# A fused attention and two-layer MoE kernel on Trainium2: other transfers for the token units, and half of MoE 2's weight preparation moved into its first pass

## The chip, the cores and the metric

The kernel runs on one core of a Trainium2 chip. The metric is the device time of one execution in microseconds (us) on that core; lower is better. Engines are named as in the profile: PE (TensorE), DVE (VectorE), ACT (ScalarE), POOL (GpSimd), SP (SyncE, which here issues DMA transfers; POOL issues some as well).

## The reference

Batch 4, 8 heads, 576 tokens, head dimension 64. Cut to what is computed:

```python
# attention: softmax over tokens pooled by 4 and repeated, plus a local softmax with |i - j| < 4
attn = np.repeat(sm_attn(q_d, k_d, v_d), 4, axis=2) + local_attn(q, k, v)
x = attn.transpose(0, 2, 1, 3).reshape(2304, 512)
# MoE 1: w_gate and w_val are 512 x 1536, w_out 1536 x 512
x = (1 / (1 + np.exp(-(x @ w_gate))) * (x @ w_val)) @ w_out
# MoE 2: w_in is 512 x 2048, w_out 2048 x 512
h = x @ w_in
g = h * np.tanh(np.log1p(np.exp(np.minimum(h, 20.0))))   # log1p(..) is h above 20
out = g @ w_out
```

## The kernel before, in words

**Numbers.** Weights are read as 64-bit numbers and narrowed to fp32 on the chip: a raw tile is loaded (`load64`), POOL or ACT makes `rebias` (L181, L179), DVE narrows in three steps (L189, L192, L196). An fp32 operand is split into `hi`, a rounded part (ACT copy, L219), and `lo`, the rest (a subtraction, L222); a product of two split operands is three matmuls.

**Blocks.** MoE 1 is done in four blocks, one per batch. Block b runs the gate and value products of batch b (`m1`, L1008 to 1010, result in `sg`, L1014) and its output products (`m1out`), and weaves in the attention of batch b + 1 (tokens come in as `tok` and `vw`) and steps of weight preparation. A planner (`weave`) sets that order, with costs, dependencies and due times: in blocks 1 and 2 a job for MoE 2's output weights (`o2`) falls due every 9500 ns, each narrowing 128 x 512 numbers, splitting them and storing both parts to `wd2` (`park_o2`); in block 3 a job for MoE 2's input weights (`i2`) every 4500 ns, 16 in all. An `i2` job also makes three sums of its quarters on POOL (L1233) and is split as 128 x 896; the jobs of the first four quads (u < `NQ`) stay in the tile `wi`, the others go to `wi2d` in device memory.

**Token units.** From four quarters of MoE 1's output, `m1out` makes seven units by additions and subtractions, for two halves `c2` of the features. `unit_out` copies a unit to `hi`, subtracts it in place to `lo`, and stores each to device memory: 256 columns to `x2d`, all batches side by side in one tensor, and, for six of the seven units, 32 rest columns to `x2r`. That is 28 + 24 stores a block. The units of `c2` = 0 lie in `stage` and a `sg` tile (`sx`), those of `c2` = 1 have their `hi` in `G`. The tiles of MoE 2 (`xu3`, `xu4`, `wo`, `g2`, `r`, `hs`, `v`) lie where `R`, `stage` and `G` were.

**MoE 2.** With seven units on each side, the product with `w_in` takes seven products instead of eight (`product`, L1332 to 1334, in the order 1, 5, 6, 2, 7, 3, 4 into `h`). MoE 2 makes two passes over halves of its hidden features: `order` is batches 0 to 3 and then the rest columns of all batches (REST, four products), and in the second pass REST first and the batches back to 0. A phase (L1395) does the products of one batch for two quads, with `mish` (L1352 to 1358) and `put_g`; between them it puts, as `units`, the output matmuls `m2out` (`po`, L1345 to 1347) of the batch before. `finish` (L1381 to 1391) stores the partial result to `pd` in the first pass; in the second it loads that into one of two `r` tiles, adds and stores the output. `follow` (L1464) loads a unit `xu` of the next batch right after its last use. `load_x2` (L1263), `load_o2` (L1253) and `load_wi` (L1256) issue on POOL's queue. `units2` (L1284) releases the pool of the weight jobs and loads the first five units of batch 0, after the last `i2` job; `xu3` and `xu4` and the `wo` tiles are loaded after block 3.

**Order.** On each engine instructions run in the order in which they stand; a scheduler lays that order out from the program's order and dependencies.

## Time and profile before

| what | us |
|---|---|
| three runs, median (lowest to highest) | 1065.14 (1056.53 to 1067.11) |
| the profiled execution | 1063.76 |
| its span, first to last instruction | 1062.0 |

The mean granted clock of PE in the profiled execution was 0.976 of full speed. Times in the rows are counted from the span's start. Blocks 0 to 3 run from about 110, 235, 380 and 525 us, MoE 2 from 652, its second pass from about 871. The time between two instructions of an engine is named idle and carries, in brackets, what released it.

### The profile page before, as it was taken

Reading aid. Unit: us, or ns where it says so; the run is one execution under the profiler, and the core shown is the slowest. Engines: PE = TensorE matmul, PEld = TensorE weight load, DVE = VectorE, ACT = ScalarE, POOL = GpSimd, SP = SyncE. Lnnn points to the kernel's source line nnn. Section 1 sums busy time; section 2 is a strip of 40 time slices with the busy share of each in tenths; the row PEclk is TensorE's granted clock in tenths of the full one; section 3 lists DMA queues with packets and bytes.
Section 4 is the critical chain, followed back from the end, with each engine's and each line's share of the span. In section 5 each row is a group of like instructions: output and inputs, shape, how many; then the busy total and the mean of one; then the engine's idle time right before and its main releaser. Section 6 shows DMA issues by size and latency. Waiting matters only on the chain.

```text
span 1062.0 us, 20544 instructions
## 1 busy us (share of the span) xinstructions
PE 988.1 (93%) x7914; PEld 920.6 (87%) x7914; DVE 694.8 (65%) x1050; ACT 578.6 (54%) x1307; POOL 340.0 (32%) x380
## 2 busy tenths in 40 slices
...
GB/s 201 178 126 221 216 193 197 180 230 237 190 214 165 164 174 169 195 172 92 146 226 159 218 270 259 293 92 172 80 99 99 139 352 151 112 217 68 152 40 100
DMA packets 165794, 184.85 MB, mean 174 GB/s; under 512 B 71104, under 2 KB 131264, under 8 KB 165184
## 3 DMA queue, kind: packets, MB, share of 16 engines
...
## 4 chain that ended last, share of the span: by engine, by line
PE 62%; DMA 15%; DVE 8%; ACT 5%; POOL 4%; issue 3%; SPq 3%; ACTq 0%; DVEq 0%; POOLq 0%
PE po L1345 6%; PE po L1347 6%; PE po L1346 6%; PE ps_m L1008 6%; PE h L1332 5%; PE h L1334 5%; PE h L1333 5%; PE ps_m L1009 5%; PE ps_m L1010 5%; PE ps_o L1052 2%; PE ps_o L1054 2%; PE ps_o L1056 2%; DMA d<-wd 2%; DMA x2d<-stage 2%; DVE R L222 2%
## 5 line engine op out<-in xcount | busy, mean ns | idle before, releaser
L1008 PE MATMUL ps_m<-R 128*128 128x288 f32 (+2 forms) x768 | 235.2, 308 | 5.7 <-DVE sg L1014 4.1
L1009 PE MATMUL ps_m<-R 128*128 128x288 f32 (+2 forms) x768 | 232.1, 302 | 2.3 <-POOL R L222 2.3
L1010 PE MATMUL ps_m<-R 128*128 128x288 f32 (+2 forms) x768 | 231.1, 301 | 0.0
L1332 PE MATMUL h<-xu,R 128*128 128x256 f32 x512 | 146.8, 287 | 13.2 <-DMA xu<-x2d 11.0
L1008 PEld LDWEIGHTS ps_m<-R 128*128 128x128 f32 x768 | 147.1, 192 | 11.2 <-DVE sg L1014 5.7
L1009 PEld LDWEIGHTS ps_m<-R 128*128 128x128 f32 x768 | 147.6, 192 | 4.0 <-POOL R L222 2.5
L1010 PEld LDWEIGHTS ps_m<-R 128*128 128x128 f32 x768 | 147.5, 192 | 1.4 <-issue 1.1
L1333 PE MATMUL h<-xu,R 128*128 128x256 f32 x512 | 146.4, 286 | 0.0
L1334 PE MATMUL h<-xu,R 128*128 128x256 f32 x512 | 146.1, 286 | 0.0
L219 ACT CAST R<-d 128x512 fp32r<-128x512 f32 (+1 forms) x152 | 95.5, 634 | 62.6 <-DVE d L214 15.9
L1052 PE MATMUL ps_o<-G,R 128*128 128x288 f32 x384 | 116.0, 302 | 0.3 <-ACT R L219 0.2
L1332 PEld LDWEIGHTS h<-xu,R 128*128 128x128 f32 x512 | 99.4, 194 | 18.4 <-DMA xu<-x2d 6.1
L1054 PE MATMUL ps_o<-G,R 128*128 128x288 f32 x384 | 114.2, 298 | 0.0
L1056 PE MATMUL ps_o<-G,R 128*128 128x288 f32 x384 | 113.5, 298 | 0.0
L1345 PE MATMUL po<-wo,g 128*128 128x512 f32 x288 | 113.2, 394 | 0.0
L1346 PE MATMUL po<-wo,g 128*128 128x512 f32 x288 | 112.7, 391 | 0.0
L1347 PE MATMUL po<-wo,g 128*128 128x512 f32 x288 | 111.0, 394 | 0.0
L222 DVE TENSOR_TENSOR R<-d,R 128x512 fp32r<-128x512 f32 (+1 forms) x118 | 90.2, 769 | 28.0 <-ACT R L219 27.2
L1333 PEld LDWEIGHTS h<-xu,R 128*128 128x128 f32 x512 | 99.5, 194 | 4.4
L1334 PEld LDWEIGHTS h<-xu,R 128*128 128x128 f32 x512 | 99.2, 194 | 0.1
L1265 POOL DMA_DIRECT2D xu<-x2d x52 | 38.9, 749 | 184.2 <-PE h L1334 177.3
L181 POOL TENSOR_SCALAR rebias<-raw 128x512 f32<-128x512 f32 x32 | 58.3, 1822 | 103.5 <-DVE d L196 80.2
...
## 6 DMA issues: line engine op xcount, KB each, us to landing
d<-wd SPq DMA_DIRECT2D x54, 512.0 KB
xu<-x2d POOLq DMA_DIRECT2D x52, 512.0 KB, 4.5
raw<-in_moe_w_out_dram SPq DMA_DIRECT2D x28, 512.0 KB
wd<-d SPq DMA_DIRECT2D x18, 512.0 KB
raw<-in_moe_w_in_dram SPq DMA_DIRECT2D x16, 512.0 KB
wo<-wd POOLq DMA_DIRECT2D x16, 512.0 KB, 6.7
...
```

The costliest lines, as they stand in the source:

```text
L1008: PE.matmul(p[:, 0:n], lhsT=wh, rhs=xh[:, c, ts], start=(c == 0), stop=False)
L1009: PE.matmul(p[:, 0:n], lhsT=wh, rhs=xl[:, c, ts], start=False, stop=False)
L1010: PE.matmul(p[:, 0:n], lhsT=wl, rhs=xh[:, c, ts], start=False, stop=(c == KD - 1))
L1052: PE.matmul(p[:, 0:SUB], lhsT=hi[:, o:o + 128], rhs=gt[:, f, 0, ts], start=(f == 0), stop=False)
L1054: PE.matmul(p[:, 0:SUB], lhsT=hi[:, o:o + 128], rhs=gt[:, f, 1, ts], start=False, stop=False)
L1056: PE.matmul(p[:, 0:SUB], lhsT=lo[:, o:o + 128], rhs=gt[:, f, 0, ts], start=False, stop=(f == KF1 - 1))
L1332: PE.matmul(o, lhsT=wh, rhs=x[:, c, 0, :], start=(start and k == 0 and c == 0), stop=False, skip_group_check=True)
L1333: PE.matmul(o, lhsT=wh, rhs=x[:, c, 1, :], start=False, stop=False, skip_group_check=True)
L1334: PE.matmul(o, lhsT=wl, rhs=x[:, c, 0, :], start=False, stop=(c == 1), skip_group_check=True)
L1345: PE.matmul(p, lhsT=gh, rhs=w[:, 0, :], start=(f == 0), stop=False)
L1346: PE.matmul(p, lhsT=gh, rhs=w[:, 1, :], start=False, stop=False)
L1347: PE.matmul(p, lhsT=gl, rhs=w[:, 0, :], start=False, stop=(f == 2 * NQ - 1))
```

## The change

The tensor `x2d` becomes one tensor per batch with 288 columns a unit, and `x2r` goes. For `c2` = 0, `hi` and `lo` of a unit are stored in one transfer each (14); for `c2` = 1 both are written side by side into `G` and stored in one (7). In blocks 1 and 2 the planner gets four `o2` jobs instead of eight, with a gap of 19000, in block 3 eight `i2` jobs instead of 16, with a gap of 8000. The other eight of each become `jobs`, done in turn by `tick`, which every product of the first pass calls: a raw tile is loaded at the fourth tick, and from the ninth on each tick does one step (rebias; narrow and next load; sums; park). They work in a new pool `sp`. The loads of `wo`, `wi` and `xu` are issued by SP; only the first seven `xu` loads of batch 0 stay on POOL. A unit of rest columns is loaded by eight transfers of 128 x 4 x 32 from the batches' tensors. The last output loop runs `a` outside `f`, with a `finish` after each `a`.

```diff
-    x2d = dram.tile([7, 128, 2, 2, B * T2], F32, name="x2d")
-    x2r = dram.tile([3, 128, 2, 2, 2, B * REM], F32, name="x2r")
+    x2d = [dram.tile([7, 128, 2, 2, SUB], F32, name="x2d%d" % b) for b in range(B)]
...
-    def unit_out(b, c2, i, d, hi):
+    def unit_out(b, c2, i, d, hi, lo):
         ACT.copy(out=hi, in_=d)
-        lo = d.bitcast(F32R)
         DVE.tensor_tensor(out=lo, in0=d, in1=hi.bitcast(F32), op=ALU.subtract)
-        for z, t in enumerate((hi, lo)):
-            t = t.bitcast(F32)
-            SP.dma_start(out=x2d[i - 1][:, c2, z, b * T2:(b + 1) * T2], in_=t[:, 0:T2])
-            if i in KIND:
-                kd, T = KIND[i]
-                SP.dma_start(out=x2r[kd][:, c2, z, T, b * REM:(b + 1) * REM], in_=t[:, T2:SUB])
...
                 h = fpool.tile([128, SUBM], F32R, tag="sg", name="sx")[:, 0:SUB]
-            else:
-                a = g6 + dd[0] * SUB
-                h = G[0][:, a:a + SUB]
-                dd[0] += 1
-            unit_out(b, c2, i, d, h)
+                unit_out(b, c2, i, d, h, d.bitcast(F32R))
+                for z, t in enumerate((h.bitcast(F32), d)):
+                    SP.dma_start(out=x2d[b][i - 1][:, c2, z, :], in_=t)
+                return
+            a = g6 + dd[0] * 2 * SUB
+            dd[0] += 1
+            h = G[0][:, a:a + 2 * SUB]
+            unit_out(b, c2, i, d, h[:, 0:SUB], h[:, SUB:2 * SUB])
+            SP.dma_start(
+                out=x2d[b][i - 1][:, c2, :, :], in_=h.bitcast(F32).rearrange("p (z t) -> p z t", z=2)
+            )
...
-    def park_o2(j, d):
-
-        hi = fpool.tile([128, 512], F32R, tag="rebias", name="hi")
-        split(d, hi, d.bitcast(F32R), DVE, late=True)
-        SP.dma_start(out=wd2[j, :, 0, :], in_=hi.bitcast(F32))
+    def src_o2(j):
+        return w2_out[j * 128:(j + 1) * 128, :].rearrange("(j p) f -> p j f", p=128), 1
+
+    def src_i2(i):
+        u, x = divmod(i, 2)
+        w = w2_in[x * 256:(x + 1) * 256, u * 256:(u + 1) * 256]
+        return w.rearrange("(j p) f -> p j f", p=128), 2
+
+    def park_o2(j, d, hi=None):
+
+        if hi is None:
+            hi = fpool.tile([128, 512], F32, tag="rebias", name="hi")
+        split(d, hi.bitcast(F32R), d.bitcast(F32R), DVE, late=True)
+        SP.dma_start(out=wd2[j, :, 0, :], in_=hi)
         SP.dma_start(out=wd2[j, :, 1, :], in_=d)
...
         done_at[0, "free"] = done_at["start"] = 0.0
-        per = KF2 // 2
+        per = KF2 // 4
         for b in range(B - 1):
...
             if b:
-                srcs = [
-                    (w2_out[j * 128:(j + 1) * 128, :].rearrange("(j p) f -> p j f", p=128), 1)
-                    for j in range((b - 1) * per, b * per)
-                ]
+                srcs = [src_o2(j) for j in range((b - 1) * per, b * per)]
                 extra += narrow_steps(
                     ("o2", b), srcs, clock[0] + 1000.0,
-                    lambda i, d, b=b: park_o2((b - 1) * per + i, d), 9500.0,
+                    lambda i, d, b=b: park_o2((b - 1) * per + i, d), 19000.0,
                 )
...
         def split_i2(i):
-            d = d7s.pop(i)
             u, x = divmod(i, 2)
-            if u < NQ:
-                split(d, wi[:, u, x, 0, :], wi[:, u, x, 1, :], DVE, late=True)
-                return
-            hi = a3.tile([128, UW], F32, tag="hi7", bufs=2, name="hi7")
+            split(d7s.pop(i), wi[:, u, x, 0, :], wi[:, u, x, 1, :], DVE, late=True)
+
+        def park_i2(i, d, hi):
+            u, x = divmod(i, 2)
             split(d, hi.bitcast(F32R), d.bitcast(F32R), DVE, late=True)
...
         def load_o2(h, j):
-            POOL.dma_start(out=wo_at[j], in_=wd2[h * 8 + j].rearrange("p z f -> p (z f)"))
+            SP.dma_start(out=wo_at[j].bitcast(F32), in_=wd2[h * 8 + j].rearrange("p z f -> p (z f)"))
         def load_wi(q):
-            POOL.dma_start(
-                out=wi[:, q].rearrange("p c z f -> p (c z f)"), in_=wi2d[q]
+            SP.dma_start(
+                out=wi[:, q].bitcast(F32).rearrange("p c z f -> p (c z f)"), in_=wi2d[q]
             )
...
-        def load_x2(t, i):
+        def load_x2(t, i, queue=SP):
             if t < B:
-                POOL.dma_start(
-                    out=xu[i - 1].rearrange("p (y t) -> p y t", y=4),
-                    in_=x2d[i - 1].rearrange("p c z t -> p (c z) t")[:, :, t * T2:(t + 1) * T2],
+                dst = xu[i - 1] if queue is POOL else xu[i - 1].bitcast(F32)
+                queue.dma_start(
+                    out=dst.rearrange("p (y t) -> p y t", y=4),
+                    in_=x2d[t][i - 1].rearrange("p c z t -> p (c z) t")[:, :, 0:T2],
                 )
             elif i <= 3:
-                POOL.dma_start(out=xu[i - 1], in_=x2r[i - 1].rearrange("p c z s t -> p (c z s t)"))
-
-        srcs = [
-            (w2_in[x * 256:(x + 1) * 256, u * 256:(u + 1) * 256].rearrange("(j p) f -> p j f", p=128), 2)
-            for u in range(FF2 // 256) for x in range(2)
-        ]
+                dst = xu[i - 1].bitcast(F32).rearrange("p (y s b t) -> p y s b t", y=4, s=2, b=B)
+                for u, (kd, T) in KIND.items():
+                    if kd == i - 1:
+                        for b in range(B):
+                            queue.dma_start(
+                                out=dst[:, :, T, b, :],
+                                in_=x2d[b][u - 1].rearrange("p c z t -> p (c z) t")[:, :, T2:SUB],
+                            )
+
         extra = weights(B - 1)
+        srcs = [src_i2(i) for i in range(2 * NQ)]
         ns = len(srcs)
-        extra += narrow_steps(("i2",), srcs, clock[0], sums_i2, 4500.0, to_i2, ahead=2)
+        extra += narrow_steps(("i2",), srcs, clock[0] + 2000.0, sums_i2, 8000.0, to_i2, ahead=2)
         for i in range(ns):
...
                 xu[i - 1] = a4[0].tile([128, XU], F32R, name="xu%d" % i)
-                load_x2(0, i)
+                load_x2(0, i, POOL)
...
         g2 = m2.tile([128, NQ * 4 * 2 * T2], F32R, name="g2")
+        sp = tc.alloc_tile_pool(name="sp", bufs=1, side="left", reuse_waits="tile")
         g2 = g2.rearrange("p (q s z t) -> p q s z t", q=NQ, s=4, z=2)
...
         for i in (3, 4):
-            load_x2(0, i)
+            load_x2(0, i, POOL)
         for j in range(2):
...
+        jobs = [z for i in range(2 * NQ) for z in ((park_i2, src_i2, 2 * NQ + i), (park_o2, src_o2, 2 * NQ + i))]
+        side, ticks = [], [0]
+        held = {}
+
+        def side_load(k):
+            held["raw"] = load64(*jobs[k][1](jobs[k][2]), sp)
+
+        def side_rebias(k):
+            held["g"] = rebias(held["raw"], POOL, sp)
+
+        def side_narrow(k):
+            held["d", k] = sp.tile([128, UW], F32, tag="d7", bufs=2, name="d7")
+            narrow(held["raw"], held["d", k][:, 0:512], held["g"])
+            if k + 1 < len(jobs):
+                side_load(k + 1)
+
+        def side_sums(k):
+            if jobs[k][0] is park_i2:
+                sums_i2(None, held["d", k])
+
+        def side_park(k):
+            hi = sp.tile([128, UW], F32, tag="hi7", name="hi7")
+            fn, _, i = jobs[k]
+            n = UW if fn is park_i2 else 512
+            fn(i, held.pop(("d", k))[:, 0:n], hi[:, 0:n])
+
+        for k in range(len(jobs)):
+            if k:
+                side.append([lambda k=k: side_park(k - 1), lambda k=k: side_rebias(k)])
+            else:
+                side.append([lambda: side_rebias(0)])
+            side.append([lambda k=k: side_narrow(k)])
+            side.append([lambda k=k: side_sums(k)])
+        side.append([lambda: side_park(len(jobs) - 1)])
+
+        def tick():
+            ticks[0] += 1
+            if ticks[0] == 4:
+                side_load(0)
+            if ticks[0] > 8 and side:
+                for fn in side.pop(0):
+                    fn()
+
         n_y = [0]
...
                     follow(k)
+                    tick()
                     if k > 1:
...
                 follow(i)
+                tick()
...
             prev = (h, t)
-        for f in range(2 * NQ):
-            for a in range(4):
+        for a in range(4):
+            for f in range(2 * NQ):
                 m2out(prev[1], f, a)
-        for a in range(4):
             finish(prev[0], prev[1], a)
```

How instructions stand now. On SP in block 1, the place where batch 2's `tok` tiles are loaded while the last units of batch 1 are stored; before, the end of it:

```order
L358 DMA tok<-in_k_dram 128x8x64
L1035 DMA x2d<-G 128x256
L1038 DMA x2r<-G 128x32
L1035 DMA x2d<-G 128x256
L1035 DMA x2d<-stage 128x256
L1038 DMA x2r<-stage 128x32
L1035 DMA x2d<-stage 128x256
L1038 DMA x2r<-stage 128x32
L1038 DMA x2r<-G 128x32
L1035 DMA x2d<-stage 128x256
L1038 DMA x2r<-stage 128x32
L1035 DMA x2d<-G 128x256
```

and with the change (`x2d_85` is batch 1's tensor):

```order
L1080 DMA x2d_85<-G 128x576 x2
L357 DMA tok<-in_k_dram 128x8x64
L1080 DMA x2d_85<-G 128x576
L249 DMA d<-wd 128x1024
L1080 DMA x2d_85<-G 128x576 x2
L357 DMA tok<-in_q_dram 128x8x64
L1080 DMA x2d_85<-G 128x576 x2
L357 DMA tok<-in_k_dram 128x8x64
L357 DMA tok<-in_q_dram 128x8x64
```

Before, 18 stores stand between a `k` and the next `q` load (the piece shows the first 11); now three.

On POOL at the start of MoE 2, before: the `xu` loads of batch 0 (units 1, 5, 6, 2, 7, then 3 and 4), the last subtractions of the units (`stage`), and `wo`:

```order
L1265 DMA xu_8327<-x2d 128x4x256
L1265 DMA xu_8329<-x2d 128x4x256
L1265 DMA xu_8331<-x2d 128x4x256
L1265 DMA xu_8333<-x2d 128x4x256
L1265 DMA xu_8335<-x2d 128x4x256
L1075 TENSOR_TENSOR stage<-stage 128x256
L1075 TENSOR_TENSOR stage<-stage 128x32
L1075 TENSOR_TENSOR stage<-stage 128x256 x2
L1265 DMA xu_8409<-x2d 128x4x256
L1265 DMA xu_8410<-x2d 128x4x256
L1253 DMA wo_8416<-wd_83 128x1024
L1253 DMA wo_8417<-wd_83 128x1024
```

With the change:

```order
L1269 DMA xu_7673<-x2d_84 128x4x256
L1269 DMA xu_7675<-x2d_84 128x4x256
L1269 DMA xu_7677<-x2d_84 128x4x256
L1269 DMA xu_7679<-x2d_84 128x4x256
L1269 DMA xu_7681<-x2d_84 128x4x256
L1067 TENSOR_TENSOR stage<-stage 128x256 x2
L1067 TENSOR_TENSOR stage<-stage 128x32
L1067 TENSOR_TENSOR stage<-stage 128x256 x4
L1067 TENSOR_TENSOR stage<-stage 128x32
L1067 TENSOR_TENSOR stage<-stage 128x256 x2
L1269 DMA xu_8047<-x2d_84 128x4x256
L1269 DMA xu_8048<-x2d_84 128x4x256
```

The five loads now stand ahead of all subtractions of block 3, where before they stood ahead of the last four.

On SP the same place with the change; the last stores of block 3 (`x2d_87`), the `wo` loads (they read `wd2`, printed as `wd_83`), the first raw tile of the side jobs and batch 1's `xu` loads:

```order
L1080 DMA x2d_87<-G 128x576 x7
L1256 DMA wo_8054<-wd_83 128x1024
L1256 DMA wo_8055<-wd_83 128x1024
L168 DMA raw<-in_moe_w_in_dram 128x2x512
L1256 DMA wo_8056<-wd_83 128x1024
L1256 DMA wo_8057<-wd_83 128x1024
L1256 DMA wo_8058<-wd_83 128x1024
L1256 DMA wo_8059<-wd_83 128x1024
L1256 DMA wo_8060<-wd_83 128x1024
L1256 DMA wo_8061<-wd_83 128x1024
L1269 DMA xu_7673<-x2d_85 128x4x256
L1269 DMA xu_7677<-x2d_85 128x4x256
```

None of these stood on SP before; the `wo` and `xu` loads come from POOL's queue, the raw tile from block 3's jobs.

On PE the last twelve matmuls, before (`po_8435` to `po_8438` are the four outputs):

```order
L1345 MATMUL po_8435<-wo7_8423,g2_8424 128x512
L1346 MATMUL po_8435<-wo7_8423,g2_8424 128x512
L1347 MATMUL po_8435<-wo7_8423,g2_8424 128x512
L1345 MATMUL po_8436<-wo7_8423,g2_8424 128x512
L1346 MATMUL po_8436<-wo7_8423,g2_8424 128x512
L1347 MATMUL po_8436<-wo7_8423,g2_8424 128x512
L1345 MATMUL po_8437<-wo7_8423,g2_8424 128x512
L1346 MATMUL po_8437<-wo7_8423,g2_8424 128x512
L1347 MATMUL po_8437<-wo7_8423,g2_8424 128x512
L1345 MATMUL po_8438<-wo7_8423,g2_8424 128x512
L1346 MATMUL po_8438<-wo7_8423,g2_8424 128x512
L1347 MATMUL po_8438<-wo7_8423,g2_8424 128x512
```

and with the change:

```order
L1355 MATMUL po_8078<-wo7_8061,g2_8062 128x512
L1356 MATMUL po_8078<-wo7_8061,g2_8062 128x512
L1356 MATMUL po_8079<-wo4_8058,g2_8062 128x512
L1354 MATMUL po_8079<-wo5_8059,g2_8062 128x512
L1355 MATMUL po_8079<-wo5_8059,g2_8062 128x512
L1356 MATMUL po_8079<-wo5_8059,g2_8062 128x512
L1354 MATMUL po_8079<-wo6_8060,g2_8062 128x512
L1355 MATMUL po_8079<-wo6_8060,g2_8062 128x512
L1356 MATMUL po_8079<-wo6_8060,g2_8062 128x512
L1354 MATMUL po_8079<-wo7_8061,g2_8062 128x512
L1355 MATMUL po_8079<-wo7_8061,g2_8062 128x512
L1356 MATMUL po_8079<-wo7_8061,g2_8062 128x512
```

Before, the four outputs end three matmuls apart; now the third ends ten before the fourth.

## Rows read from the trace of the kernel before

**Rows 1.** Busy time, share and instructions of each engine, from the page.

```profile
PE 988.1 (93%) x7914; PEld 920.6 (87%) x7914; DVE 694.8 (65%) x1050; ACT 578.6 (54%) x1307; POOL 340.0 (32%) x380
```

**Rows 2.** Waits of PE: line, tile, releaser: us in total, times, longest.

```profile
PE h L1332 <- DMA xu<-x2d: 11.0, 2, 5.7
...
PE ps_t L449 <- DMA tok<-in_q_dram: 6.6, 2, 3.7
...
PE ps_m L1008 <- DVE sg L1014: 4.1, 6, 1.3
```

**Rows 3.** Stretches: PE, PEld, DVE, ACT, POOL busy (instructions), PE clock, DMA share, GB/s.

```profile
400.00:405.00 5.00, 5.00 (x29) 4.80 (x29) 1.19 (x3) 2.40 (x5) 0.00 (x0) 0.66 1.12 279
540.00:595.00 55.00, 50.39 (x364) 48.30 (x363) 50.22 (x82) 28.58 (x59) 39.59 (x41) 1.00 0.50 163
...
652.00:660.00 8.00, 2.64 (x12) 2.26 (x11) 0.95 (x2) 0.82 (x2) 5.75 (x8) 0.81 1.07 264
...
689.00:695.00 6.00, 5.95 (x30) 5.96 (x31) 1.23 (x1) 1.96 (x3) 0.17 (x1) 0.55 1.80 346
...
700.00:871.00 171.00, 171.00 (x1053) 153.18 (x1052) 94.45 (x90) 91.86 (x113) 18.74 (x29) 1.00 0.45 137
```

**Rows 4.** SP's DMA issues from 380 to 396: start, us, line, transfer.

```profile
380.39 0.55 SPq L1035 DMA_DIRECT2D x2d<-stage  x1
...
395.38 0.41 SPq L358 DMA_DIRECT2D tok<-in_q_dram  x1
```

**Rows 5.** Groups by line and shape: busy, mean ns, idle before and releasers.

```profile
L181 POOL TENSOR_SCALAR rebias<-raw 128x512 f32<-128x512 f32 x32 | 58.3, 1822 | 103.5 <-DVE d L196 80.2 <-DVE sum L495 10.8 <-DMA raw<-in_moe_w_in_dram 6.7
...
L1233 POOL TENSOR_TENSOR d<-d 128x128 f32<-128x128 f32 x64 | 45.0, 724 | 21.0 <-DVE d L196 16.4 <-PE ps_m L1010 2.7 <-ACT R L219 1.1
...
L189 DVE TENSOR_SCALAR d<-rebias 128x512 int32<-128x512 int32 x38 | 22.4, 590 | 16.7 <-DMA wd<-d 11.0 <-POOL R L222 2.7 <-ACT rebias L179 1.4
...
L192 DVE SCALAR_TENSOR_TENSOR d<-raw,d 128x512 int32<-128x512 int32 x38 | 30.7, 808 | 0.3
...
L222 DVE TENSOR_TENSOR d<-d,hi 128x896 fp32r<-128x896 f32 x8 | 8.9, 1118 | 3.4 <-ACT hi L219 3.2
...
L222 DVE TENSOR_TENSOR d<-d,hi 128x512 fp32r<-128x512 f32 x16 | 11.1, 691 | 12.5 <-ACT hi L219 12.5
```

**Rows 6.** PE's timeline at MoE 2's first product and at batch 1's first.

```profile
657.77 0.55 PE L1332 MATMUL h<-xu,R 128*128 128x256 f32 x1 [5.36 <-DMA xu<-x2d]
...
689.05 0.58 PE L1332 MATMUL h<-xu,R 128*128 128x256 f32 x1 [5.68 <-DMA xu<-x2d]
```

**Rows 7.** POOL's timeline around the start of MoE 2.

```profile
652.57 3.91 POOL L1265 DMA_DIRECT2D xu<-x2d  x5 [2.11 <-DMA wi2d<-d]
...
680.10 1.65 POOL L1253 DMA_DIRECT2D wo<-wd  x3 [12.03 <-DVE e L1354]
```

**Rows 8.** The chain that ended last, 668 to 698: start, us, what.

```profile
668.63 10.84 DMA x2d<-stage
...
695.03 0.12 PE h L1333
...
697.54 0.23 PE po L1346
```

**Rows 9.** Timeline of the end: PE's last matmul and DVE's last add.

```profile
1054.06 0.39 PE L1347 MATMUL po<-wo,g 128*128 128x512 f32 x1
...
1057.96 0.69 DVE L1389 TENSOR_TENSOR o<-po,r 128x512 f32<-128x512 f32 x1 [0.60 <-DMA r<-pd]
```

**Rows 10.** DVE's split into G, 530 to 610, then 380 to 525: min/median/max ns.

```profile
L222 DVE TENSOR_TENSOR G<-sg,G x21: 439/704/891, 541.2 to 609.8; 128x288 fp32r<-128x288 f32 x21
...
L222 DVE TENSOR_TENSOR G<-sg,G x24: 405/450/1469, 387.8 to 491.5; 128x288 fp32r<-128x288 f32 x24
```

**Rows 11.** Issues of `vw` on SP (ns), and loads of the rest columns (us to landing).

```profile
L378 SPq DMA_DIRECT2D vw<-in_v_dram x80: 595/608/2015, 5.3 to 471.4; - x80
...
xu<-x2r POOLq DMA_DIRECT2D x3, 512.0 KB, 3.6
```

10 lines of the change are left out of this document (6 added, 4 removed).

## Prediction

> **What bounds the kernel now.** I read the page's busy times first, then the waits of PE, then the stretches, and last the timelines of the places where PE stood. PE is busy 988.1 us of a span of 1062.0 [rows 1], so the change can win only the other 74 us, plus what PE runs at the lower of its two clock levels. The waits of PE name three places that this change touches [rows 2]: token loads of attention (6.6 us in two waits), the first MoE's matmuls behind DVE's `sg` (4.1 us in six), and MoE 2's first products behind `xu` loads (11.0 us in two). The stretches [rows 3] show the rest. From 540 to 595 DVE is busy 50.2 of 55 us and PE only 50.4. Around the start of MoE 2 PE does 2.64 us of work in 8 (652 to 660), and from 689 to 695 it is fully busy at a granted clock of 0.55, near 1.2 GHz instead of 2.4. In MoE 2's first pass (700 to 871) PE never stops, with DVE busy 94.45 of 171, 55%: there nothing can be won and something can be lost.
>
> **The change part by part.** The sum is made against the profiled execution, 1063.8 us (span 1062.0); the median of the three runs is 1065.1, the lowest 1056.5.
>
> *Fewer, longer unit stores.* A block issued 28 + 24 stores and now issues 21; the 24 small ones go. Between 380.39 and 395.38 SP issued 24 of them one after the other [rows 4], 0.6 us apart, and PE's second token wait (up to 3.7 us) ends with that token load. In the new order seven stores from `G` stand where 24 stood, so the load can go some 10 us earlier, far more than the wait. What is saved is at most both waits, 6.6, and the low clock right behind the second (5 us at 0.66 [rows 3], 1.7 us of work lost): 8.3. At least 0, if the token loads then wait for their buffers. I take 6.
>
> *Half of MoE 2's weight preparation leaves blocks 1 to 3.* In block 3 a job came every 4.5 us of the planner's time and now comes every 8. A job costs DVE 0.59 + 0.81 + 0.79 + 1.12 = 3.3 us (the third, L196, is like L192, its row is left out) [rows 5]. In 55 us that is 12 jobs before and 7 after, 16 us less, so DVE falls from 91% to about 62%, near the level of MoE 2 where PE did not wait. PE's idle 4.6 us there [rows 3] should go: 4.5, between 0 and 4.6.
>
> *Start of MoE 2.* Now: the last matmul of MoE 1 ends at 657.77 - 5.36 = 652.4, and PE waits for `xu1`, whose load POOL issues at 652.57 after a wait for a `wi2d` store [rows 6, 7]. `xu3` and `xu4` come behind stage subtractions. Then eight `wo` loads, of which POOL issues the last three only at 680.10, after standing 12.03 us; the row names a DVE instruction on `e`, which no `wo` load touches, and what lands just before is an `x2d` store from `stage`, after 10.84 us [rows 7, 8]. Behind those three stand the `xu` loads of batch 1, and PE starts batch 1 at 689.05 after 5.68 us [rows 6]. From 652.4 to 689.05 are 36.65 us, for 14 products of 12 matmuls at 0.12 us and five `po` matmuls at 0.23 [rows 8], 21.3 us of work. After: the five loads of batch 0 wait for no store of block 3 and stand on POOL ahead of the last subtractions, some 45 us early, so the first wait goes. What is late next is DMA: behind the last matmul lie seven stores (2.0 MB), `xu3` and `xu4` (1.0), eight `wo` (4.0), one raw tile (0.5) and `xu1` of batch 1 (0.5), 8 MB in all. At 346 GB/s, the rate of 689 to 695 [rows 3], that is 23 us, and with 2 us until the first lands batch 1 starts 25.5 us after the last matmul instead of 36.65: 11.1 saved. If the clock stays up, the 2.7 us lost from 689 to 695 (6 us at 0.55) come back too; of these I give 1.3 back for the later `xu` loads, 1.5 us apart. 12.5 us. Lower end: only the first wait and the low clock behind it go, 5.4 + 3.3 = 8.7. Upper end: PE's work alone, 15.3 + 2.7 less 2 for gaps, 16.
>
> *Last outputs.* The last DVE add starts at 1057.96, and PE's last matmul ended at 1054.06 + 0.39 = 1054.45 [rows 9]: 3.5 us, because the third and fourth `r` tile are loaded only when the first two adds free their buffers. In the new order the outputs end 7, 10 and 10 matmuls apart, so the second is done 20 x 0.23 = 4.6 us before the last; its add, two issues and a landing, with the 3.6 us of rows 11, fill about 5. Saved 3.2, between 0 and 3.5. The matmuls that hide the last activation are as many as before (59 rows against 57 up to the first late one), so that wait does not grow.
>
> *The other half of the preparation, now beside MoE 2's first pass.* 16 jobs, of which 8 with a split of 512 columns (0.69 us): 8 x 3.3 + 8 x 2.9 = 49.5 us on a DVE that has 94.45 of 171 busy: 144, 84%. POOL adds 16 rebias of 1.82 us and 32 small sums of 0.72, 52 us [rows 5]. DVE instructions get longer beside a busy POOL: the split of 128x288 had a median of 704 ns from 530 to 610 and 450 from 380 to 525 [rows 10]; POOL was 72% busy from 540 to 595 [rows 3]. With POOL at 30% of the first pass (52 of 171) and some 112 instructions of this kind, 0.25 us each at 30/72 makes 12 us more, DVE 91%. At 91% PE lost 4.6 of 55 us [rows 3], which over 171 is 14. At 55% it lost nothing. So 0 to 14; between the two estimates of the load I take 6.
>
> *The queue.* 45 loads of `xu`, `wo` and `wi` leave POOL (0.74 us for an `xu`) for SP, where each costs 0.3 to 0.6 us [rows 11]. Nothing in the first pass waits for them now: an `xu` tile is freed in one phase and read in the next but one half, some 20 us later, and lands in about 5 (652.57 to 657.77). So 0, while SP keeps moving. But SP runs in order, and behind an `xu` load that waits for PE now stand the raw tiles that POOL and DVE need, the `pd` stores that free `o`, and in the second pass the `r` loads. That cover is what two of the rivals take away.
>
> *Loads for the rest columns.* Three loads of 512 KB (3.6 us each) become 24 of 64 KB in pieces of 128 bytes. The nearest row is `vw`, 64 KB in pieces of 256 bytes, 0.6 us of SP each [rows 11]: a unit needs 8 x 0.6 = 4.8 us plus a landing of about 3.5. The tightest is `xu3`: 28 `po` and 36 `h` matmuls, 10.7 us, between its last use and its next. That fits if `xu2`'s eight are through by then. 0 to 8, the upper end if each unit's landing follows the one before; I take 1.
>
> Sum: -6 - 4.5 - 12.5 - 3.2 + 6 + 1 = -19.2, so 1044.6.
>
> **The rivals.** *Only the first wait goes.* `wo` and `g2` lie where `R`, `stage` and `G` were, and the raw tile on SP waits for all seven `G` stores, with six `wo` and batch 1's `xu` behind it. If that hole and the DMA load keep batch 1 as late as now, the start gives 8.7, and with 7 for the first pass it is 1063.8 - 6 - 4.5 - 8.7 - 3.2 + 7 = 1048. For it: the raw load's place. Against it: the 12.03 us in which POOL stood before the last `wo` loads are gone.
>
> *The first pass gives most of it back.* The full 14 of the 91% row, 8.7 at the start and 3 at the rest columns: 1063.8 - 6 - 4.5 - 8.7 - 3.2 + 14 + 3 = 1058, no change that counts. If POOL's 52 us came wholly on top of DVE's 144, that would be 196 in a pass of 171, 25 too many, and 1063.8 - 6 - 4.5 - 12.5 - 3.2 + 25 + 1 = 1064. For it: the 540 to 595 stretch is just such a mix. Against it: products in MoE 2 are spaced by `po` matmuls, which need nothing from DVE in that moment.
>
> The Trainium skill (SBUF — State Buffer, Who interferes with whom) has a rule for the second of these: a VectorE instruction with two SBUF inputs is shut out by a GpSimd instruction that reads SBUF until that is done, not merely slowed. The trace agrees in sign, with 254 ns at the median [rows 10]; a whole rebias of 1.82 us per instruction it does not show.
>
> *The rest columns hold PE.* If `xu3`'s eight loads start only when `xu2`'s have landed, that is 2 x (4.8 + 3.5) = 16.6 us against the 10.7 there are: 6 of stall instead of 1, 1050. The Trainium skill (DMA: Bandwidth & Descriptors, Rules for kernel authors) speaks for it: transfers under 64 KB are mostly overhead and should be made one. No run here shows such a load yet.
>
> *Slower: raw tiles late behind SP.* DVE runs in order too. A narrowing step waits for POOL's rebias, that for the raw tile, that for an SP that stands at an `xu` load until PE is through. Then DVE holds the activation that PE needs, and PE stands. The other terms win 26.2 with the rest columns at 0, so this decides from 26.2 / 16 = 1.6 us per job. At 2.5 us a job it costs 40: 1063.8 - 26.2 + 40 = 1078. For it: SP alternates `xu` and raw loads all through the pass. Against it: a raw tile is asked for two products, some 6 us, ahead.
>
> **How the numbers follow.** Forecast as summed (1034 to 1052) 0.55; only the first wait 0.15; given back 0.17; rest columns 0.05; slower 0.05; all parts at their good ends, 1063.8 - 32.4 = 1031, 0.03. Faster by over 1% means under 1054.5, about what a measurement of this kernel tells from no change: all but given back, slower and a hundredth of the others, 0.77. Within 1%: 0.18, slower 0.05. The range leaves out the slower case, the worst of given back and the best: 1032 to 1060.
>
> **What the changed profile would show.** Right: no PE wait for `tok` of over 1 us near 250 and 400; no wait for `sg` from 540 to 595; the first product within 1 us of MoE 1's last matmul, at clock 1.00; batch 1 about 25 us behind; the last DVE add within 0.5 us of the last matmul. Wrong: PE below 95% in the first pass, with DVE named as releaser behind rebias or raw; a PE wait for `xu` at the rest columns; `xu1` of batch 1 later than 30 us. The forecast falls if the first pass loses over 15 us.

## The result and the profile after

| | us |
|---|---|
| changed kernel, four runs, median (lowest to highest) | 1029.97 (1025.27 to 1032.60) |
| kernel before, four runs beside them | 1061.56 (1056.53 to 1067.11) |
| ratio, 95% interval | 0.9696 (0.9625 to 0.9768) |
| profiled execution of the changed kernel, its span | 1032.60, 1030.8 |

The change brings 31.6 us by the medians and 31.2 between the two profiled spans, where 19.2 were forecast; 1030 lies under the range of 1032 to 1060. First the busy times, which answer to [rows 1]:

```profile
PE 978.9 (95%) x7914; PEld 912.9 (89%) x7914; DVE 689.3 (67%) x1050; ACT 579.4 (56%) x1307; POOL 294.7 (29%) x312
```

PE runs as many matmuls, 7914, and is 9.2 us less busy: that part of the gain is not waiting. Much of it goes with the clock, whose mean rose from 0.976 to 0.987; how much in blocks 1 and 2, the last section works out. The waits of PE that answer to [rows 2], from the list of the changed kernel:

```profile
PE h L1341 <- ACT h L1478: 3.1, 2, 2.0
...
PE h L1341 <- DVE h L1484: 1.4, 2, 1.0
PE h L1341 <- DVE hs L1490: 1.4, 2, 1.1
...
PE h L1341 <- DMA xu<-x2d: 1.4, 1, 1.4
...
PE po L1354 <- ACT o L1392: 1.1, 1, 1.1
```

The waits for `tok` and for DVE's `sg` are gone from the list; the small waits of MoE 2's products for ACT and DVE have grown. To see where the time went, I cut both traces at the same matmuls. PE's n-th matmul stands at nearly the same work in every kernel, so the difference of two start times, stage by stage, is what the stage won. The cuts are matmul 1950 (239.0 us in the kernel before), 4650 (530.5), 5480 (647.5), 5720 (696.8) and 6560 (832.8); the last matmul starts at 1054.06 before and at 1026.39 now, and what follows it took 7.9 us and takes 4.4. The stretches of before (new here but for what [rows 3] showed) with these cuts:

```profile
239.00:382.00 143.00, 138.87 (x1353) 133.13 (x1352) 102.23 (x206) 83.96 (x263) 41.77 (x38) 0.99 0.65 192
382.00:530.50 148.50, 140.73 (x1351) 135.12 (x1351) 95.08 (x197) 80.59 (x253) 30.12 (x23) 0.98 0.51 157
530.50:647.50 117.00, 112.39 (x832) 110.30 (x831) 99.05 (x158) 56.59 (x115) 80.33 (x88) 1.00 0.65 217
647.50:696.80 49.30, 36.13 (x243) 34.72 (x242) 19.94 (x26) 21.05 (x35) 18.17 (x27) 0.86 1.11 293
696.80:832.90 136.10, 136.10 (x843) 122.06 (x842) 81.83 (x79) 77.89 (x96) 11.98 (x17) 1.00 0.34 93
```

and the same five of the changed kernel (columns as in [rows 3]: PE, PEld, DVE, ACT, POOL busy, then PE's clock, DMA share, GB/s):

```profile
242.20:379.00 136.80, 136.80 (x1353) 131.72 (x1352) 90.59 (x187) 81.13 (x255) 34.93 (x35) 1.00 0.55 159
379.00:514.80 135.80, 135.55 (x1352) 130.82 (x1352) 87.69 (x182) 78.87 (x250) 26.02 (x22) 1.00 0.46 145
514.80:624.80 110.00, 110.00 (x833) 110.00 (x832) 70.06 (x122) 50.54 (x108) 38.42 (x50) 1.00 0.51 156
624.80:661.90 37.10, 32.48 (x243) 31.02 (x242) 21.88 (x28) 22.24 (x35) 6.52 (x8) 0.97 0.91 310
661.90:805.30 143.40, 137.89 (x842) 122.26 (x842) 113.67 (x136) 83.39 (x107) 54.25 (x47) 1.00 0.67 210
```

Blocks 1 and 2, the first two rows, fell by 6.2 and 12.7 us. Of these 18.9 us PE's idle time was 11.6 (4.1 + 7.8 - 0.3) and its busy time for as many matmuls 7.3 (279.6 against 272.35), some 5 of it the clock. Block 3 won 7.0, the start of MoE 2 12.2, the first pass gave back 7.3, and the end won 3.5. Up to matmul 1950, counted from PE's first, the changed kernel was 3.1 us behind, mostly at the start, where a first stretch at the lower clock lasted 17 us instead of 10; of the profiles that follow, one a kernel, some show it, some not, with the same instructions there.

```
us won (-) or lost against the kernel before, by stage of PE's matmuls, profiled executions
                 to    1950 to  4650 to  5480 to  5720 to  6560 to    ratio to before (95%)
                 1950  4650     5480     5720     6560     the last
changed           3.1  -19.0    -7.0    -12.1      7.4    -0.1       0.9696 (0.9625 to 0.9768)
changed_again    -1.0  -18.0    -7.0    -13.2      5.8    -0.1       0.9658 (0.9626 to 0.9690)
e1_stores        -1.8   -9.6    -5.5     -5.1     -0.9     0.3       0.9858 (0.9803 to 0.9914)
e9_28_stores      3.4   -9.2    -2.8     -4.3     -1.0     0.3       0.9908 (0.9873 to 0.9942)
f2_o2_half       -2.1  -11.1    -2.3      0.2      0.0     0.8       0.9928 (0.9897 to 0.9959)
e5_old_stores    -2.9   -8.2    -6.8     -7.3      4.9     1.3       0.9813 (0.9777 to 0.9850)
e2_o2_back        2.4  -13.2    -7.0    -11.9      4.0    -0.1       0.9779 (0.9730 to 0.9828)
e3_i2_back       -2.4  -17.8    -4.1     -6.0      0.0    -0.1       0.9754 (0.9703 to 0.9806)
e4_no_side       -2.1   -9.3    -3.2     -2.2     -0.1     0.2       0.9821 (0.9764 to 0.9878)
e6_pool_queue     0.2  -19.0    -7.0    -11.8      2.9     0.7       0.9670 (0.9631 to 0.9709)
e8_tick_late     -1.4  -18.3    -7.0    -13.7      5.5     0.2       0.9675 (0.9622 to 0.9727)
f1_both          -0.2  -19.1    -7.0    -12.3      3.9     0.9       0.9689 (0.9624 to 0.9753)
f3_rest_split     2.8  -19.1    -7.0    -11.8      4.4    -0.2       0.9668 (0.9602 to 0.9734)
f5_raw_ahead     -2.6  -19.1    -7.0    -13.9     34.3     1.3       0.9946 (0.9914 to 0.9978)
f4_two_raw        5.0  -19.1    -7.0    -13.1     25.3     0.4       0.9866 (0.9824 to 0.9907)
f6_two_hi        -2.7  -18.8    -7.0    -13.9     32.7     1.3       0.9953 (0.9925 to 0.9981)
f8_hi_only        3.8  -18.6    -7.0    -13.2      3.6    -0.1       0.9701 (0.9659 to 0.9744)
```

The table holds all kernels that follow. Its third column is blocks 1 and 2, its fourth block 3, then the start of MoE 2 and the first pass. Where the same program stands in two kernels (blocks 1 to 3 of the changed kernel, its second run and the last eight) the columns of blocks 1 to 3 agree within 1.1 us. They need not: through block 2 the kernels e1_stores, e2_o2_back and e4_no_side have the same instructions in the same order on every engine, and won 9.6, 13.2 and 9.3 us; through block 3 e1_stores and e4_no_side have, and won 5.5 and 3.2 in it. So a difference of 2 to 4 us between two single profiles is not told apart, and all lines stand against one profile of the kernel before. The ratios, with intervals of 0.006 to 0.015, do not show the stages.

The end, which answers to [rows 9]; PE's last matmul and DVE's last add:

```profile
1026.39 0.39 PE L1356 MATMUL po<-wo,g 128*128 128x512 f32 x1
```

```profile
1026.82 0.69 DVE L1398 TENSOR_TENSOR o<-po,r 128x512 f32<-128x512 f32 x1 [1.41 <-PE po L1356]
```

The last add starts at 1026.82, 0.04 us after PE's end (1026.39 + 0.39), where it stood 3.5 us behind.

### The profile page after: what moved, and what is told of

It reads as the page before. It is cut to its first block, busy times and chain, and to the rows that moved or that the text cites. A ratio compares the mean times of both kernels' runs of the same rounds, so it can differ in the third digit from the quotient of the medians.

```text
span 1030.8 us, 20419 instructions
## 1 busy us (share of the span) xinstructions
PE 978.9 (95%) x7914; PEld 912.9 (89%) x7914; DVE 689.3 (67%) x1050; ACT 579.4 (56%) x1307; POOL 294.7 (29%) x312
## 4 chain that ended last, share of the span: by engine, by line
PE 67%; DMA 11%; DVE 8%; ACT 5%; POOL 4%; issue 3%; SPq 1%; POOLq 0%; ACTq 0%; DVEq 0%
PE ps_m L1007 9%; PE ps_m L1008 9%; PE ps_m L1009 8%; PE po L1356 4%; PE po L1354 4%; PE po L1355 4%; PE ps_o L1044 4%; PE ps_o L1046 4%; PE ps_o L1048 4%; PE h L1341 4%; PE h L1343 4%; PE h L1342 4%; DMA raw<-in_moe_w_out_dram 2%; DMA raw<-in_moe_w_in_dram 2%; POOL d L1237 2%
## 5 line engine op out<-in xcount | busy, mean ns | idle before, releaser
L1341 PEld LDWEIGHTS h<-xu,R 128*128 128x128 f32 x512 | 97.6, 191 | 15.4 <-ACT h L1478 4.4
L1342 PEld LDWEIGHTS h<-xu,R 128*128 128x128 f32 x512 | 97.7, 191 | 4.2
L1343 PEld LDWEIGHTS h<-xu,R 128*128 128x128 f32 x512 | 97.6, 191 | 0.3
L1044 PEld LDWEIGHTS ps_o<-G,R 128*128 128x128 f32 x384 | 72.5, 189 | 2.7 <-ACT R L218 2.1
```

The source lines that it names most:

```text
L1044: PE.matmul(p[:, 0:SUB], lhsT=hi[:, o:o + 128], rhs=gt[:, f, 0, ts], start=(f == 0), stop=False)
L1341: PE.matmul(o, lhsT=wh, rhs=x[:, c, 0, :], start=(start and k == 0 and c == 0), stop=False, skip_group_check=True)
L1342: PE.matmul(o, lhsT=wh, rhs=x[:, c, 1, :], start=False, stop=False, skip_group_check=True)
L1343: PE.matmul(o, lhsT=wl, rhs=x[:, c, 0, :], start=False, stop=(c == 1), skip_group_check=True)
```

## The experiments

**What won in blocks 1 and 2: stores or jobs.** Theory Q says that the stores on SP held all that stands behind them, theory D that the eight `o2` jobs fewer made room. Stores alone:

```diff
-    x2d = dram.tile([7, 128, 2, 2, B * T2], F32, name="x2d")
-    x2r = dram.tile([3, 128, 2, 2, 2, B * REM], F32, name="x2r")
+    x2d = [dram.tile([7, 128, 2, 2, SUB], F32, name="x2d%d" % b) for b in range(B)]
...
+            SP.dma_start(
+                out=x2d[b][i - 1][:, c2, :, :], in_=h.bitcast(F32).rearrange("p (z t) -> p z t", z=2)
+            )
```

> The kernel before with the new stores alone (a tensor per batch, 21 transfers a block, rest columns read from the batches' tensors by SP); all preparation, POOL's loads and the last outputs as before. Between the profiles blocks 1 and 2 won some 16 to 19 us (from 3 us behind at PE's matmul 1650 to 15.7 ahead at matmul 4050), where the prediction had 6. Theory Q (SP's queue): SP, with 31 transfers a block fewer, brings all that stands behind them earlier, token tiles and weights too; then this kernel wins nearly all of it, 14 to 19 us by matmul 4050, nothing in block 3, up to 5 at the start of MoE 2, in all 14 to 24 us under before, ratio 0.977 to 0.987. Theory D (DVE): the four o2 jobs that each of blocks 1 and 2 lost made room on DVE, and the waits for its El, xn and sg went with them; then this kernel wins the two token waits, 6 us, and what lies at the start, in all 6 to 11, ratio 0.990 to 0.994.

Measured: 9.6 us in blocks 1 and 2, 5.1 at the start, 15.0 in all by the ratio (0.9858). The total is theory Q's, the stages are neither's: the stores won more than the two token waits, but half of what blocks 1 and 2 won (two more profiles of these instructions come below). And the kernel won 5.5 us in block 3, where nothing was expected. The waits of PE in block 2 before, with stores alone, and with jobs alone (the kernel after next):

```profile
PE ps_t L449 <- DMA tok<-in_q_dram: 3.7, 1, 3.7
PE ps_l L685 <- DVE El L693: 2.4, 1, 2.4
PE ps_la L792 <- DVE xn L811: 1.7, 1, 1.7
```

```profile
PE ps_la L791 <- issue: 1.4, 1, 1.4
PE ps_g L541 <- ACT Eg L554: 0.9, 1, 0.9
PE ps_t L448 <- DMA tok<-in_q_dram: 0.2, 1, 0.2
```

```profile
PE ps_l L685 <- DVE El L693: 1.7, 1, 1.7
PE ps_t L449 <- DMA tok<-in_q_dram: 1.7, 1, 1.7
```

The token wait went with the stores, as forecast, and of the two waits for DVE the one for `El`. Where PE had waited for `xn` it still stood 1.4 us, for nothing that the profile names, and in block 1 of this kernel a wait of 2.1 us for `xn` is new.

Fewer stores, with `lo` left in `stage`:

```diff
+            unit_out(b, c2, i, d, h, d.bitcast(F32R))
+            for z, t in enumerate((h.bitcast(F32), d)):
+                SP.dma_start(out=x2d[b][i - 1][:, c2, z, :], in_=t)
```

> The kernel before with a tensor per batch and no small stores: 28 a block, hi and lo of every unit apart, lo left in stage for both halves as before; rest columns as in the stores-alone kernel. If the number of transfers that SP issues decides, it has 24 of the 31 that go: three quarters or more of what stores alone won, 1044 to 1048. Rival (what decides is that lo of the second half lies in G, so that no later write to stage waits for its store): half or less of it, 1052 to 1058.

Measured: 9.2 us in blocks 1 and 2, where 21 stores won 9.3 to 13.2; in block 3 2.8, where they won 3.2 and 5.5. By the ratio it has 9.7 of the 15 us; the total fell between the two expectations. So in blocks 1 and 2 most of what the stores won is there without the 24 small transfers. What merging `hi` and `lo` adds is within the spread of the profiles, and the tensor per batch, which both kernels have, was not tried alone.

The jobs alone:

```diff
-        per = KF2 // 2
+        per = KF2 // 4
...
-                    lambda i, d, b=b: park_o2((b - 1) * per + i, d), 9500.0,
+                    lambda i, d, b=b: park_o2((b - 1) * per + i, d), 19000.0,
...
-            POOL.dma_start(out=wo_at[j], in_=wd2[h * 8 + j].rearrange("p z f -> p (z f)"))
+            POOL.dma_start(out=wo_at[j], in_=wd2[j].rearrange("p z f -> p (z f)"))
```

> The kernel before with one edit: four o2 jobs in each of blocks 1 and 2 instead of eight, a gap of 19000. The other eight jobs are left out, and the second pass reads the first half's output weights again, so it computes another product there; its work is the same. The prediction priced these jobs at nothing in blocks 1 and 2. If their room on DVE, POOL and SP is the second half of what those blocks won, this kernel wins 7 to 9 us between matmul 1950 and 4050, nothing over 2 behind that: 1049 to 1052, ratio 0.990 to 0.994. Rival (the gain needs the new stores too, or the token waits only move): under 3 us, ratio 0.997 or more.

Measured: 11.1 us in blocks 1 and 2, ratio 0.9928 (7.6 us of its median). This is the gain that the prediction priced at nothing. Blocks 1 and 2 together, before and then this kernel:

```profile
239.00:530.50 291.50, 279.60 (x2702) 268.26 (x2701) 197.31 (x403) 164.55 (x514) 71.88 (x61) 0.98 0.58 174
```

```profile
237.30:517.70 280.40, 274.55 (x2701) 263.55 (x2701) 178.49 (x368) 159.98 (x503) 60.20 (x55) 1.00 0.50 150
```

DVE does 18.8 us less, POOL 11.7, PE waits 6.1 us less (11.9 to 5.9) and is 5.0 us less busy, at a clock of 1.00 instead of 0.98. Whether DVE's room, POOL's, or the three transfers that each job takes from SP is what counts, no run separates.

The changed kernel with old stores, and with the `o2` jobs back:

```diff
-    x2d = [dram.tile([7, 128, 2, 2, SUB], F32, name="x2d%d" % b) for b in range(B)]
+    x2d = dram.tile([7, 128, 2, 2, B * T2], F32, name="x2d")
+    x2r = dram.tile([3, 128, 2, 2, 2, B * REM], F32, name="x2r")
```

> The changed kernel with the 52 stores a block, the shared tensor x2d and x2r of before (rest columns in one load a unit); all else changed. From the first four runs: stores alone won 9 to 10 us between matmul 1950 and 4050, 4 to 5 in block 3; halving the o2 jobs another 8 in blocks 1 and 2. Theory Q (the stores on SP, and what stands behind them): this kernel loses 9 to 10 in blocks 1 and 2, 3 to 5 in block 3, and up to 5 at the start of MoE 2, where SP now also carries wo and xu: 1043 to 1050. Rival (the room that the moved jobs leave on DVE and SP makes up for the stores): it loses under 6: 1030 to 1036.

```diff
-        per = KF2 // 4
+        per = KF2 // 2
...
-        jobs = [z for i in range(2 * NQ) for z in ((park_i2, src_i2, 2 * NQ + i), (park_o2, src_o2, 2 * NQ + i))]
+        jobs = [(park_i2, src_i2, 2 * NQ + i) for i in range(2 * NQ)]
```

> The changed kernel with all 16 o2 jobs in blocks 1 and 2 as before (eight a block, a gap of 9500); beside the first pass only the eight i2 jobs. Theory Q: blocks 1 and 2 stay as fast as in the changed kernel (within 3 us by matmul 4050), and the first pass, with half the jobs, gives back 4 less: 1026, 0 to 5 us under the changed kernel. Theory D: blocks 1 and 2 lose 9 to 10 of their 16 again, the first pass gives back 4 less: 1035, some 5 above it.

Measured: with old stores blocks 1 and 2 keep 8.2 of 19.0, with the old number of jobs 13.2. Through block 2 the first has the instructions of the jobs-alone kernel and the second those of the stores-alone kernel, as has the kernel without side jobs below. So these blocks won 9.3, 9.6 and 13.2 with the stores alone, 8.2 and 11.1 with the jobs alone, and 17.8 to 19.1 in the eleven profiles that have both: within that spread the two edits add up (17.5 to 24.3). The total with old stores, 1041, is just under what theory Q expected, since block 3 kept its gain. The second came out at 1035.5, where theory D had 1035, though the blocks lost 5.8 and not 9 to 10.

**Block 3 and the start of MoE 2.** The `i2` jobs back in block 3, and then all preparation back:

```diff
-        srcs = [src_i2(i) for i in range(2 * NQ)]
+        srcs = [src_i2(i) for i in range(4 * NQ)]
...
-        extra += narrow_steps(("i2",), srcs, clock[0] + 2000.0, sums_i2, 8000.0, to_i2, ahead=2)
+        extra += narrow_steps(("i2",), srcs, clock[0], sums_i2, 4500.0, to_i2, ahead=2)
```

> The changed kernel with all 16 i2 jobs in block 3 as before (a gap of 4500); beside the first pass only the eight o2 jobs. Both theories: block 3 loses its 7 us again, the five xu loads stand behind the last i2 job once more, so up to 5 at the start of MoE 2, and the first pass gives back 4 to 5 less: 1030 to 1040. Rival (block 3 won by the stores too, not by DVE): block 3 keeps over half of its 7 us, and the kernel is no slower than the changed one.

```diff
+        per = KF2 // 2
...
+        srcs = [src_i2(i) for i in range(4 * NQ)]
...
-        jobs = [z for i in range(2 * NQ) for z in ((park_i2, src_i2, 2 * NQ + i), (park_o2, src_o2, 2 * NQ + i))]
+        jobs = []
```

> The changed kernel with all preparation in the blocks as before, nothing beside the first pass; stores, SP's loads and the last loop stay changed. It prices the side jobs: the first pass (matmul 5720 to 6560) should take what it took before, some 8 us less than in the changed kernel, if the side jobs are what it lost, and keep the loss if SP's queue or the rest columns' loads are. Theory Q: blocks 1 and 2 keep their gain, block 3 loses 7, the start up to 5: 1030 to 1036. Theory D: 9 more lost in blocks 1 and 2: 1040 to 1046.

Measured: with all 16 `i2` jobs block 3 still won 4.1, 3.2 and (stores alone) 5.5 us of the 7.0, and 2.3 with the `o2` jobs halved and old stores; with old stores and half the `i2` jobs 6.8. Here the edits do not add up: halving the `i2` jobs takes away nearly all of the waits, the stores a part of the same ones, and at 7.0 PE has none left. With stores alone DVE is as loaded as before, yet in this profile PE hardly waits. The kernel without side jobs, which has the same instructions through block 3, follows:

```profile
519.00:595.00 76.00, 75.66 (x564) 74.69 (x563) 70.74 (x117) 39.80 (x84) 58.15 (x63) 1.00 0.63 210
```

```profile
519.00:595.00 76.00, 73.66 (x547) 72.36 (x546) 67.70 (x113) 38.67 (x81) 57.40 (x61) 1.00 0.60 204
```

DVE is busy 70.74 of 76, 93%, and PE stands 0.3 us; in the second DVE is at 89% and PE stands 2.3; in [rows 3] DVE at 91% stood beside 4.6 us of idle PE. The second's waits in the block:

```profile
PE ps_m L1007 <- DVE sg L1013: 1.6, 1, 1.6
PE ps_m L1007 <- ACT sg L1012: 0.7, 2, 0.4
```

One difference from the kernel before stands on POOL, before and then with stores alone:

```profile
531.26 0.73 POOL L1075 TENSOR_TENSOR stage<-stage 128x256 f32<-128x256 f32 x1 [9.20 <-DMA x2d<-stage]
```

```profile
516.75 0.79 POOL L1067 TENSOR_TENSOR stage<-stage 128x256 f32<-128x256 f32 x1 [6.69 <-ACT stage L1055]
```

Before, POOL stood 9.2 us for a store of `stage` that SP had not got to, and the `i2` jobs of block 3 queued behind it; it went on 0.8 us after block 3 began (530.5). With the new stores it went on 2.7 us before (519.4). But so it did in the kernel without side jobs, whose PE waited 2.3 us; that POOL's place is the cause is not shown. The start lost 6.1 us with the `i2` jobs back (6.0 instead of 12.1): the early loads of `xu` need half of them. The first pass lost nothing without side jobs and nothing with the eight `o2` jobs alone, with SP's loads and the 24 rest loads in place: neither of these costs anything by itself. With the eight `i2` jobs alone (the `o2` jobs back) it lost 4.0: the loss goes with the `i2` jobs. Theory D's total for the kernel without side jobs (1040 to 1046) was met at 1041.9.

**What the first pass gives back.** Two edits, each by itself and then both:

```diff
-            SP.dma_start(out=wo_at[j].bitcast(F32), in_=wd2[h * 8 + j].rearrange("p z f -> p (z f)"))
+            POOL.dma_start(out=wo_at[j], in_=wd2[h * 8 + j].rearrange("p z f -> p (z f)"))
...
-        def load_x2(t, i, queue=SP):
+        def load_x2(t, i, queue=POOL):
```

> The changed kernel with xu, wo and wi loaded by POOL again (rest columns and raw tiles by SP). If SP's queue is part of what the start of MoE 2 won, wo and batch 1's xu stand on POOL behind its last subtractions and beside the rebias steps: batch 1 starts 30 us or more after MoE 1's last matmul instead of 25, and the kernel is 3 to 8 us slower, 1033 to 1038. Rival (the start was won by the five early xu loads alone, which the halved i2 jobs allow): within 2 us of the changed kernel. In the first pass neither expects a difference over 2 us.

```diff
                     if units:
                         units.pop(0)()
+                tick()
...
                 follow(i)
-                tick()
```

> The changed kernel with each side step written after the copy or addition and the output matmuls that follow a product, no longer ahead of them. In the changed kernel the waits in the first pass are for h and hs, which DVE makes behind three narrowing steps or ACT behind the mish steps; with 8 o2 jobs alone the pass lost nothing, with 8 i2 jobs 4 us, with all 16 7 to 9. If the place of the steps is what costs, PE's waits there fall from 7.5 us to under 4: 1024 to 1027. Rival (the sum of work on DVE and ACT is what costs): within 2 us of the changed kernel.

> The changed kernel with both later edits: xu, wo and wi on POOL, and the side steps behind the copies. Alone the first cut what the first pass lost (matmul 5720 to 6560) from 7.4 to 2.9, the second to 5.5, of which 3 at the rest columns. If they cut different waits, the pass loses under 3 and the kernel takes 1020 to 1024. Rival (they cut the same waits, or POOL's rebias steps now stand behind its loads): no less than with POOL's queue alone, 1025 to 1028.

Measured: the pass gives back 2.9 with POOL's queue, 5.5 with late steps, 3.9 with both, and 7.4 and 5.8 in the two profiles of the changed kernel (the second is below). With late steps PE's waits in the pass came to 3.0 us, under the 4 of that theory, 2.4 of them for `xu` at the rest columns. The start was the same with POOL's queue (11.8 against 12.1 and 13.2): the queue was no part of that gain, which goes to the halved jobs and the stores. By the ratios none of the three can be told from the changed kernel. With both edits one wait makes up the loss, and it is the one that the prediction's slower case described, once, not per job; PE's row, DVE's and POOL's:

```profile
739.01 0.58 PE L1341 MATMUL h<-xu,R 128*128 128x256 f32 x1 [3.83 <-DVE hs L1489]
```

```profile
737.93 0.43 DVE L188 TENSOR_SCALAR d<-rebias 128x512 int32<-128x512 int32 x1 [3.92 <-POOL rebias L180]
```

```profile
736.39 1.51 POOL L180 TENSOR_SCALAR rebias<-raw 128x512 f32<-128x512 f32 x1 [9.30 <-DMA raw<-in_moe_w_in_dram]
```

DVE stands at a narrowing step for a rebias, that for a raw tile, and PE's `hs` stands behind it. Three kernels followed from this: with both edits and rest loads on two queues; the changed kernel with raw tiles two jobs ahead; and all of these together. The changed kernel was run once more beside the last two.

```diff
-                            SP.dma_start(
+                            (SP, POOL)[b % 2].dma_start(
```

> As the kernel with both edits, and the 24 rest loads go to SP and POOL in turn. PE's wait for xu at the rest columns was 1.35 us in the changed kernel, 1.37 and 2.38 in the two edited ones. If SP's issue of eight loads a unit is what holds it, the wait goes: 1 to 3 us less than with both edits alone. Rival (the loads' landing holds it, or rebias steps now wait behind POOL's rest loads): the same within 1 us, or more.

```diff
-            held["raw"] = load64(*jobs[k][1](jobs[k][2]), sp)
+            held["raw", k] = load64(*jobs[k][1](jobs[k][2]), (sp, fpool)[k % 2])
...
-            if k + 1 < len(jobs):
-                side_load(k + 1)
+            if k + 2 < len(jobs):
+                side_load(k + 2)
```

> The changed kernel once more, beside the two below on one chip: the same as at first, 0.965 to 0.975 of the kernel before; in the first pass (matmul 5720 to 6560) 6 to 9 us lost against it.

> The changed kernel with the side jobs' raw tiles loaded two jobs ahead, in turn into the pool sp and into the blocks' old raw buffer. Theory R (the pass loses to raw tiles that come late behind SP's xu loads, so that POOL's rebias and then DVE stand): the pass loses under 3 us instead of 6 to 9, 3 to 6 us faster than the changed kernel. Rival W (it loses to the side steps' own work on DVE and ACT ahead of what PE needs): within 2 us of it.

> The kernel with both edits and rest loads on two queues, and raw tiles two jobs ahead. There PE's one long wait in the pass was 3.8 us for hs on DVE, which stood 3.9 us behind a rebias, which stood 9.3 us for a raw tile, with a low clock after it. Theory R: that goes, the pass loses under 1 us, 1018 to 1023. Rival W: waits of 1 to 2 us stay elsewhere, 1023 to 1027.

Measured: the split rest loads changed nothing that can be told (0.9668 against 0.9689, the intervals overlap). In neither is a wait for `xu` left at the rest columns. The changed kernel came to 0.9658, as expected, and lost 5.8 us in the pass, just under the 6 to 9 expected. Raw tiles ahead made the pass 27 us slower than in the changed kernel (34.3 against 7.4), and 21 slower with the other edits (25.3 against 4.4): theory R fell, and W, which expected no difference, with it. PE stands there for ACT's `hs` copies:

```profile
PE h L1341 <- ACT hs L1494: 14.0, 4, 7.3
PE h L1341 <- ACT hs L1487: 7.3, 2, 5.3
```

In the second profile of the changed kernel all its waits in the pass come to 4.5 us. The clock adds to that: 0.92 of full speed over the pass with raw tiles ahead, 1.00 in the changed kernel, and PE is 9.9 us longer busy (147.13 against 137.22). The waits of ACT around the pass, raw tiles ahead and then the changed kernel (second profile):

```profile
ACT hi L218 <- POOL d L1237: 19.3, 7, 6.5
...
ACT hi L218 <- DMA wi2d<-hi: 7.5, 2, 4.6
ACT o L1392 <- DMA pd<-o: 6.2, 4, 3.2
```

```profile
ACT hi L218 <- POOL d L1237: 13.0, 7, 4.1
...
ACT hi L218 <- DMA wi2d<-hi: 2.5, 2, 1.6
```

ACT stands longer at its casts, for POOL's sums and for the store of the job before, and the `hs` copies come behind them in its order. The second of these could be taken away:

```diff
-            hi = sp.tile([128, UW], F32, tag="hi7", name="hi7")
+            if fn is park_i2:
+                hi = sp.tile([128, UW], F32, tag="hi7", name="hi7")
+            else:
+                hi = fpool.tile([128, 512], F32, tag="d2", bufs=1, name="d2")
```

> The changed kernel with raw tiles two jobs ahead, as in the run that lost 34 us in the first pass, and now a hi tile of its own for each kind of job, so that ACT's cast no longer waits for the store of the job before. Theory S: there the jobs ran up against that store; ACT stood 4 to 5 us at a cast, behind SP's issue and landing of the store before, with the copies of h that PE needs behind it. Then the pass loses under 12 us instead of 34: 1030 to 1038. Rival P (it is SP's place of the pd stores, for which ACT's copies of po wait, and DVE's crowding): it still loses over 24: 1046 or more.

> The changed kernel with a hi tile of its own for each kind of job and nothing else. If the store of the job before also holds ACT in the changed kernel, the pass loses 2 to 4 us less than its 6 to 9: 1023 to 1026 beside 1027 to 1030. Rival: raw tiles pace the jobs there, so the cast comes after that store in any case: within 1.5 us of the changed kernel.

Measured: with a `hi` of its own ACT's wait for that store is gone and the pass still lost 32.7 us, so theory S fell; P's number was met, its cause is not shown. In the changed kernel the pass lost 3.6, less than in its two profiles, but the ratio (0.9701) is no better. Why earlier raw tiles cost so much stays open: POOL's sums, which ACT still waits for, and SP's later `pd` stores are both left, and neither was tried alone.

## Why the prediction was wrong

**The step that failed** is the term for the stores, "What is saved is at most both waits, 6.6, and the low clock right behind the second", 8.3 at most and 6 taken, together with the next heading, "Half of MoE 2's weight preparation leaves blocks 1 to 3", under which only block 3 was priced. Blocks 1 and 2 won 19.0 (18.0 in the second profile). By the rows this is three things. Waits that were in the list of waits, but for which no edit seemed responsible: `El` 2.4, `xn` 1.7 and, in block 1, `sg` 1.1 us, 5.2 in all. PE's busy time: 7.3 us less, some 5 of it the clock in three stretches, where one of 1.7 was counted. And the token waits themselves in full, 6.6. That makes 19.1, with 0.3 us of idle time left. The runs show which edits did it: the stores alone won 9.3 to 13.2 us, more than the 8.3 named as the most, and the `o2` jobs alone, priced at nothing here, 8.2 and 11.1; together that is what the change got. What of a job counts, its time on DVE, on POOL or on SP, stays open. The jobs' cost on DVE was worked out under block 3 (3.3 us each) and never laid beside the DVE waits of blocks 1 and 2.

**Right in size, partly in cause.** The start of MoE 2: 12.1 and 13.2 against 12.5. Batch 1's first product starts at 654.69, 25.3 us after the last matmul ahead of MoE 2's products (629.01 + 0.39), where 25.5 were worked out (23 and 2 are 25); PE's timeline, and that stretch:

```profile
629.01 0.39 PE L1325 MATMUL h<-R 128*128 128x512 f32 x1
...
654.69 0.28 PE L1341 MATMUL h<-xu,R 128*128 128x256 f32 x1
...
629.40:654.70 25.30, 22.66 (x176) 21.72 (x177) 14.02 (x17) 13.50 (x20) 5.78 (x7) 1.00 1.02 353
```

The wait for the first `xu` went, as forecast. The DMA moved at the rate that was taken, 353 GB/s against 346, but it was not what PE waited for: PE was busy 22.66 us, and its 2.6 us of idle time were three waits for copies of `h` and `hs` on ACT and DVE (0.7, 0.7, 1.0) and one of 0.3 for `stage`, none for `xu`. That PE's own work and the transfers of the prediction both come to about 25 us is luck.

The last outputs are right in size and cause: 3.5 against 3.2, with the last add right behind PE's end. The low clock after MoE 2's first wait is nearly gone (0.97 over the stage instead of 0.86).

**Right in size, not wholly in cause.** Block 3 won 7.0 against 4.5: all of PE's idle time, 4.6, and 2.4 us of busy time at a clock of 1.00 before and after, which no term had. Halving the `i2` jobs does bring it (6.8 with old stores). But DVE's share does not set the wait by itself: with the new stores and all 16 jobs PE waited 0.3 us in one profile, with DVE at 93%, and 2.3 in another of the same instructions, at 89%; what decides there is not shown. The first pass gave back 7.4 and 5.8, against 6 and 1 for the rest columns. For the pass as the prediction bounds it, DVE did 132 us of work, where 144 were worked out, in 178.9 us, 74%: under both estimates (84 and 91). At the rest columns PE did wait for `xu`, 1.4 us, the one sign of being wrong that showed; but these loads cost nothing by themselves (0.0 and -0.1 us lost in the two kernels that keep the 24 without `i2` side jobs), and SP's queue, priced at nothing "while SP keeps moving", may have: with POOL's queue the pass lost 2.9.

**The rivals.** None came. One put POOL's 52 us wholly on top of DVE's. POOL was busy 54 us in the pass, but what DVE's instructions beside POOL took above the median of the same ones without it comes to an estimated 3.5 us. The narrowing steps with two inputs had means of 686 and 685 ns there:

```profile
L195 DVE SCALAR_TENSOR_TENSOR d<-rebias,d 128x512 int32<-128x512 int32 x15 | 10.3, 686 | 0.2
L191 DVE SCALAR_TENSOR_TENSOR d<-raw,d 128x512 int32<-128x512 int32 x15 | 10.3, 685 | 0.2
```

None of these 30 ran beside a POOL instruction: the rebias stands before them and the sums behind. So they do not test the Trainium skill's rule (SBUF — State Buffer, Who interferes with whom) that a VectorE instruction with two SBUF inputs contends with a GpSimd instruction that reads SBUF. The kernel before does, in the same steps (L192 and L196; minimum, median and maximum in ns):

```profile
L192 DVE SCALAR_TENSOR_TENSOR d<-raw,d x38: 677/684/2175, 27.9 to 635.2; 128x512 int32<-128x512 int32 x38
L196 DVE SCALAR_TENSOR_TENSOR d<-rebias,d x38: 675/682/2752, 28.6 to 637.0; 128x512 int32<-128x512 int32 x38
```

The 53 of these 76 with nothing on POOL beside them took 675 to 696 ns; of the other 23, ten took under 700 and 13 took 779 to 2752. The trace agrees with the rule there, and shows more than the 254 ns of [rows 10]. What the rival had wrong is how often the two meet.

The slower case, raw tiles late behind SP, showed as one wait of 3.8 us, in a kernel of the experiments. The "best" case, all parts at their good ends, gave 1031 and a chance of 0.03; it named the right time for another reason, since the first pass was not at its good end.
